# Turning a block of x by DMA by head pairs, and moving the loads of batch 2 behind it

## The chip, the cores and the metric

The kernel runs on one core of one Trainium2 chip. The metric is the device time of one execution in microseconds (us); lower is better. A core has five engines with their own instruction streams: TensorE (PE, the matrix engine; its weight loads are shown as PEld), VectorE (DVE), ScalarE (ACT), GpSimd (POOL) and SyncE (SP). In this kernel SP issues nearly all DMA transfers, and POOL issues most stores of the output.

## The reference

```python
def attn(q, k, v):                     # (8 batches, 8 heads, 576 rows, 64)
    cos, sin = cos/sin(pi/2 * pos / S)
    phi = lambda x: concat([relu(x) * cos, relu(x) * sin], -1)
    kv  = einsum('bhsf,bhsd->bhfd', phi(k), v)
    z   = sum(phi(k), axis=2)
    num = einsum('bhsf,bhfd->bhsd', phi(q), kv)
    den = einsum('bhsf,bhf->bhs', phi(q), z)[..., None] + 1e-06
    return num / den

def moe(x, w_in, w_out, beta):         # x (4608, 512), w_in (512, 2048)
    h = x @ w_in
    g = h * sigmoid(beta * h)
    return g @ w_out                   # (4608, 512)

x = attn(q, k, v).transpose(0, 2, 1, 3).reshape(4608, 512)
out = moe(x, w_in, w_out, beta)
```

## The kernel before

The 4608 tokens are worked on in two tilings at once. The attention goes by batch (8 batches of 576 rows); the two large products go by chunk (9 chunks of 512 tokens). A batch is held as 9 blocks of 64 tokens (n = 0 to 8), with two groups of 64 rows on the 128 partitions, and four head pairs, of which two by two make one of two pair halves (`jp` 0 and 1). A chunk takes 8 blocks: chunk 0 takes batch 0's blocks 0 to 7; chunk 1 takes batch 0's block 8 and batch 1's blocks 0 to 6; chunk 2 begins with batch 1's blocks 7 and 8.

For each batch:

- `load_raw(b, name)` loads q, k or v as float32 on SP's queue (1152 KB each) into one buffer per name, so a load waits until the batch before has been read.
- `q_relu`, `k_relu`, `v_scale` make the bf16 operands: relu of q and k, and v times the cosine and times the sine of the position (`vb`, one row of instructions per block).
- `q_turn_pe` or `q_turn_dma` turns q so that features lie on the partitions (`qts`), by PE or by a DMA transpose; a product with the tangent (`tan_mul`) makes the sine part `qs`.
- `kv_mm` (L276) makes the key-value product in PSUM, `kv_take` copies it out.
- `num_mm` (L297) makes numerator and denominator; `x_rden` (L308, L312) takes the reciprocal of the denominator, and `x_mul` (L319) writes x in bf16 to `xs`.
- `x_turn_pe` (L356, with copies L361 and L363) or `x_turn_dma` (L367) turns x into the chunk's tile `xt`, one tile of 8 blocks by two pair halves.

For each chunk, `h_group` runs 4 matmuls of 512 columns (`h_mm`, L386: two for each pair half) and one activation (`h_act`, L394) for each of 16 column tiles of w_in; then the output product follows. Chunk 0's output is made in the plain way (`o_mm`, L543), chunk 1's and later ones with seven block products in place of eight, which need differences of w_out (`T1` to `T4`, `w_sums`) and sums of g (`S1` to `S4`). `T3` takes the place of a part of w_out that chunk 0's output reads.

The order of the work is written out by hand. Every engine runs its instructions in the order in which they are emitted, and so does SP's queue of DMAs. The slots concerned are these: 32 slots of chunk 0 (4 to 15 finish h, 16 to 31 make the output; slots 24 to 31 take one of the last 8 tiles each) with the dictionary `early` of what is put behind a slot for batch 1; then the 16 slots of chunk 1's h, with the preparation of batch 2 between; then the output of chunk 1 (`o_fast`), with batch 2's numerators and the relu of batch 3's q. Matmuls of a slot go to banks of PSUM (8 of 2 KB) that are named by hand: chunk 1's first four h groups take banks 6, 7, 4, 5, later ones 0, 1, 4, 5 in turn; chunk 0's last outputs are in banks 2, 3, 0, 1.

In the kernel before, batch 1's blocks 0 to 6 are turned by PE (seven transposes at slot 28, seven at slot 29), all three loads of batch 2 are issued at slot 24, and batch 2's key-value product stands behind chunk 1's group 10.

Of the kernel before, what the change touches and what calls it, by code (L numbers as in the profile page):

```python
# [16 lines left out]
P = 128  # L17
# [5 lines left out]
def kernel(  # L23
# [52 lines left out]
    def load_raw(b, name, j0=0, j1=4):  # L76
        js = slice(j0, j1)
        src = {"q": q, "k": k, "v": v}[name][b]
        nc.sync.dma_start(  # L79
            out=raw_tile(b, name)[:, js].rearrange("q j n d -> q j (n d)"),  # L80
            in_=src.rearrange("(j g) (p n) d -> (g p) j (n d)", g=2, n=NQ)[:, js, :])
# [35 lines left out]
    def cast_out(j, eng="d"):  # L117
        i, jj = divmod(j, 4)
        st = stages["out", i]
        if eng == "a":  # L120
            nc.scalar.activation(wout[:, j, :], st[:, jj, :], AF.Copy, scale=rbeta[:, j : j + 1])
        else:
            nc.vector.tensor_scalar(wout[:, j, :], st[:, jj, :],
                                    scalar1=rbeta[:, j : j + 1], scalar2=None, op0=ALU.mult)
# [46 lines left out]
    qs_first = one.tile([P, 2, NQ, P], BF16, name="qs")  # L171
    kv = one.tile([P, 2, 2, 2, E], BF16, name="kv")
    xs = one.tile([P, NQ, 2, 2 * D], BF16, name="xs")

    nc.vector.reciprocal(eps9, cos9)
    nc.vector.tensor_tensor(tan9, eps9, sin9, op=ALU.mult)
# [113 lines left out]
    def num_mm(b, n, jp, bank, slot):  # L290

        for cs in range(2):
            for jj in range(2):
                rows = slice(jj * HP, (jj + 1) * HP)
                for g in range(2):
                    cols = slice(g * HP, (g + 1) * HP)
                    nc.tensor.matmul(  # L297
                        ps[cols, bank + jj, slot * E : (slot + 1) * E],
                        lhsT=(qts[b % 2], qs_of(b))[cs][rows, jp, n, cols],
                        rhs=kv[rows, g, jp, cs, :],  # L300
                        start=(cs == 0), stop=(cs == 1))

    def x_rden(bank, slot, n0, n1, jps):

        w, m = len(jps), n1 - n0
        nv = ps[:, bank : bank + 2, slot * E : (slot + w * m) * E].rearrange("q j (i s e) -> q j i s e", s=w, e=E)
        den = small.tile([P, 2, m, w], FP32, name="den", tag=f"den{m}{w}")
        nc.vector.tensor_tensor(  # L308
            den, nv[:, :, :, :, D],
            eps9[:, n0:n1].unsqueeze(1).unsqueeze(3).to_broadcast([P, 2, m, w]), op=ALU.add)  # L310
        rden = small.tile([P, 2, m, w], FP32, name="rden", tag=f"rden{m}{w}")
        nc.vector.reciprocal(rden, den)  # L312
        return nv, rden, n0, jps

    def x_mul(got, n0, n1):
        nv, rden, first, jps = got
        a, z, w = n0 - first, n1 - first, len(jps)
        o = xs[:, n0:n1, jps[0] : jps[-1] + 1].rearrange("q n s (j d) -> q j n s d", j=2)
        nc.vector.tensor_tensor(  # L319
            o.rearrange("q j n s d -> q j (n s) d"),  # L320
            nv[:, :, a:z, :, 0:D].rearrange("q j n s d -> q j (n s) d"),
            rden[:, :, a:z].rearrange("q j n s -> q j (n s)").unsqueeze(3).to_broadcast([P, 2, (z - a) * w, D]),
            op=ALU.mult)
# [27 lines left out]
    def x_turn_pe(b, n0, n1, bank, engs=("act",), jps=(0, 1)):  # L351
        m, w = n1 - n0, len(jps)
        tv = ps[:, bank].bitcast(BF16)[:, 0 : w * m * P].rearrange("q (n s c) -> q n s c", n=m, s=w)
        for i in range(m):
            for s_, jp in enumerate(jps):
                nc.tensor.matmul(tv[:, i, s_, :], lhsT=xs[:, n0 + i, jp, :], rhs=ident, is_transpose=True,  # L356
                                 start=(i == 0 and s_ == 0), stop=(i == m - 1 and s_ == w - 1))
        for k_, (c, o, a, z) in enumerate(pieces(b, n0, n1)):
            dst, src = xt_tile(c)[:, o : o + z - a, jps[0] : jps[-1] + 1], tv[:, a - n0 : z - n0]
            if engs[k_ % len(engs)] == "act":  # L360
                nc.scalar.copy(dst, src)  # L361
            else:
                nc.vector.tensor_copy(dst, src)  # L363

    def x_turn_dma(b, n0, n1):
        for c, o, n0, n1 in pieces(b, n0, n1):
            nc.sync.dma_start(out=xt_tile(c)[:, o : o + n1 - n0].rearrange("q n s c -> q (n s) c"),  # L367
                              in_=xs[:, n0:n1].rearrange("q n s c -> q (n s c)"), transpose=True)


    gs = {}
# [50 lines left out]
    def wx_tiles():  # L422

        wx["w"] = stage.tile([P, 4, 512], FP32, name="w_stage", tag="w_stage").rearrange("q a f -> q (a f)").bitcast(
            BF16).rearrange("q (k s g f) -> q k s g f", k=4, s=4, g=2)
        wx["v"] = stage.tile([P, 4, 512], FP32, name="w_stage", tag="w_stage").rearrange("q a f -> q (a f)").bitcast(
            BF16).rearrange("q (k s g f) -> q k s g f", k=4, s=4, g=2)
        wx["x"] = stage.tile([P, 4, 512], FP32, name="w_stage", tag="w_stage").rearrange("q a f -> q (a f)").bitcast(
            BF16).rearrange("q (s n c) -> q s n c", s=8, n=NB // 2)
        wx["q"] = stage.tile([P, 4, 512], FP32, name="w_stage", tag="w_stage").rearrange("q a f -> q (a f)").bitcast(  # L430
            BF16)[:, 0 : 2 * NQ * P].rearrange("q (s n c) -> q s n c", s=2, n=NQ)
# [352 lines left out]
    def num_seven(jp, bank):  # L784
        for n in range(7):
            num_mm(1, n, jp, bank, n)
# [3 lines left out]
    def second():  # L790

        takes.append(q_turn_pe(1, 0, 4, hold=True))
        takes.append(q_turn_pe(1, 1, 6, hold=True))
        cast_out(8)
        takes[0]("act", 0)
        takes[0]("dve", 1)
        cast_out(9, "a")
        takes[0]("dve", 0)
        takes[0]("act", 1)
        cast_out(10)  # L800
        for e, i in (("act", 0), ("dve", 1), ("act", 1), ("dve", 0)):
            takes[1](e, i)
        for j in (11, 12, 14, 15):
            cast_out(j, "a")

    early = {
# [1 line left out]
        15: lambda: (v_scale(1, 1, n1=8, eng="act"), k_relu(1, 2, 4, "act")),  # L808
        22: lambda: (kv_mm(1, 0, 6), kv_mm(1, 1, 6), kv_take((0, 1), 6, "act"), q_relu(1, 1, "act", 5)),
        23: second,  # L810
        25: lambda: (num_seven(0, 4), x_mul(x_rden(4, 0, 0, 7, (0,)), 0, 7), cast_out(13)),
        26: lambda: (num_seven(1, 6), x_mul(x_rden(6, 0, 0, 7, (1,)), 0, 7)),
        28: lambda: x_turn_pe(1, 0, 7, 4, ("act",), (0,)),
        29: lambda: x_turn_pe(1, 0, 7, 5, ("dve",), (1,)),
    }

    def num_rest():
        for n in range(7, NQ):
            for jp in range(2):
                num_mm(1, n, jp, 2, 2 * (n - 7) + jp)  # L820
        x_mul(x_rden(2, 0, 7, NQ, (0, 1)), 7, NQ)
        x_turn_dma(1, 7, NQ)

    def att_q(b, turn=True):
        q_relu(b, 0)
# [23 lines left out]
    def x_part(b, t, bank):  # L849
        x_div(t, bank)  # L850
        x_turn_dma(b, 3 * t, 3 * t + 3)

    for slot in range(32):
        if slot < 4:
            if slot == 0:
                for jt in range(2):
                    h_mm(0, jt, (2, 3), slice(0, 4))
            h_mm(0, slot, (2, 3), slice(4 if slot < 2 else 0, 8))
            h_act(0, slot)
        elif slot < 16:  # L860
            h_group(0, slot)
        elif slot < 24:
            o_part(0, slot % 4, (slot - 16) // 4)
        else:
            for tt in range(4):
                o_mm(0, tt, (slot - 16,))
        if slot == 24:
            for name in "qvk":
                load_raw(2, name)
        if slot in early:  # L870
            early[slot]()

    def w_sums():
        z = ALU.subtract
        nc.vector.tensor_tensor(T1, B12, B11, op=z)
        nc.vector.tensor_tensor(T2, B22, T1, op=z)
        nc.vector.tensor_tensor(T4, B21, T2, op=z)
        nc.vector.tensor_tensor(T3, B22, B12, op=z)

    wx_tiles()  # L880
    for slot in range(16):
        h_group(1, slot)
        if slot == 0:
            num_rest()
            att_q(2)
            v_half(2, 0)
        if 2 <= slot < 6:
            v_half(2, 1, slot + 3, slot + 4, "act")
        if slot == 4:
            k_all(2)  # L890
            v_half(2, 1, 0, 5)
        elif slot == 6:
            w_sums()
        elif slot == 10:
            kv_all(2, eng="act")
            for jp in range(2):
                tan_mul(nc.vector, qs_of(2)[:, jp], qts[0][:, jp], 0, NQ)
    q_relu(3, 0, "act")
    q_relu(3, 1, "act")
    q_turn_dma(3)  # L900

    def one_sums(kind):
        for i0 in range(0, JT // 2, 2):
            g_sum(1, i0, i0 + 2, kind)
# [6 lines left out]
    ops(x, "1 c1")  # L911
    one_sums(1)
    ops(y, "1 c1")
    for t, bank in enumerate((4, 6, 0)):
        num_all(2, t, bank)
    one_sums(2)
# [174 lines left out]
```

## Time and profile before

| | |
|---|---|
| median of 3 runs | 274.5 us (274.12 to 275.24) |
| span of the profiled execution, first to last instruction | 272.8 us |
| PE busy | 265.6 us (97%) |
| DVE busy | 224.3 us (82%) |
| ACT busy | 188.6 us (69%) |
| POOL busy | 67.5 us (25%) |
| mean granted TensorE clock | 0.999 |

The profile gives the span and no separate device time of that execution; the median of the runs is 1.7 us above the span. Times in the timelines count from the first instruction. Busy times are of one profiled execution; "L356" is line 356 of the kernel before. A DMA instruction's own time is the time SP took to issue it; when its data have landed is told apart, as "us to landing" from the issue.

### The profile page before, as it was taken

To read this page: it belongs to the slowest core of one execution; us is meant where nothing else is said; L and a number is where in the kernel's file an instruction comes from. 1 tells how busy PE (TensorE), PEld (TensorE's weight loads), DVE (VectorE), ACT (ScalarE), POOL (GpSimd) and SP (SyncE) were. 2 spreads that over 40 slices of the span, in tenths; PEclk is the share of its full clock that TensorE was granted. 3 is DMA by queue.
4 is the path that set the end of the run, shared out by engine and by line. 5 is a ranking of instruction groups with operands and counts; after the bars stand their busy time and mean duration, and the time that the engine had idled before them with its cause. 6 is when DMAs were issued, how large, how long until landed. Compare 5 with 4: busy or idle time off the path is not lost.

```text
span 272.8 us, 8972 instructions
## 1 busy us (share of the span) xinstructions
PE 265.6 (97%) x3712; PEld 207.0 (76%) x3712; DVE 224.3 (82%) x596; ACT 188.6 (69%) x384; POOL 67.5 (25%) x87
## 2 busy tenths in 40 slices
PE   8889999999999999999999999999999999999993
PEld 8554455445874488888888888888888888888882
DVE  5889959499999989789989996999599768748841
ACT  4778777797329656899489967996695179329910
POOL 1454000510078000560094009300930060000000
PEclk9999999999999999999999999999999999999999
DMA  7999999999959999893689339944500460024006
GB/s 221 388 390 377 394 390 312 394 207 344 278 114 331 215 362 258 264 296 67 190 210 353 85 63 244 293 70 83 162 1 8 77 163 2 2 47 110 0 6 151
DMA packets 50745, 54.00 MB, mean 198 GB/s; under 512 B 31232, under 2 KB 31760, under 8 KB 50704
## 3 DMA queue, kind: packets, MB, share of 16 engines
q1 hardware_dynamic: 47664, 45.82, 59.1%
q0 software_dynamic: 2688, 7.34, 9.2%
q8 instruction: 29, 0.48, 0.7%
q10 hardware_dynamic: 352, 0.27, 0.4%
q14 instruction: 12, 0.10, 0.1%
HBM read 36.71 MB, written 9.44 MB: 169 GB/s over the span
## 4 chain that ended last, share of the span: by engine, by line
PE 91%; DMA 3%; DVE 2%; SPq 1%; issue 1%
PE ps L620 32%; PE ps L511 27%; PE ps L386 15%; PE ps L543 5%; PE ps L562 5%; PE ps L297 4%; DMA raw_v<-in_v_dram 3%; PE ps L276 3%; DVE xs L319 1%; SPq L79 1%; PE ps L356 0%; PE ps L235 0%; DVE win L115 0%; DVE rden L312 0%; DVE vb L209 0%
## 5 line engine op out<-in xcount | busy, mean ns | idle before, releaser
L420 ACT ACTIVATE g_t<-ps,beta 128x512 bf16<-128x512 f32 x96 | 60.4, 704 | 1.4 <-PE ps L511 1.3
L536 POOL DMA_DIRECT2D out_dram<-o_sb x56 | 32.9, 594 | 103.7 <-ACT o_sb L657 44.0
L620 PEld LDWEIGHTS <-S 128*128 128x128 bf16 x448 | 43.4, 98 | 5.2
L511 PE MATMUL ps<-w_stage 128*128 128x256 bf16 x288 | 46.6, 272 | 0.1
L386 PE MATMUL ps<-xt,win 128*128 128x512 bf16 (+1 forms) x196 | 42.8, 375 | 0.1
L511 PEld LDWEIGHTS <-w_stage 128*128 128x128 bf16 x384 | 37.3, 98 | 5.1 <-issue 0.3
L487 DVE TENSOR_TENSOR ps<-ps,p 128x256 f32<-128x256 f32 x74 | 30.5, 427 | 8.6 <-PE ps L511 3.0
L394 ACT ACTIVATE g_t<-ps,beta 128x512 bf16<-128x512 f32 x48 | 32.3, 689 | 7.2 <-PE ps L386 7.1
L620 PEld LDWEIGHTS <-g_t 128*128 128x128 bf16 x336 | 32.3, 98 | 4.5 <-ACT g_t L420 0.4
L386 PEld LDWEIGHTS <-win 128*128 128x128 bf16 x196 | 18.8, 98 | 21.0 <-issue 0.4
L511 PE MATMUL ps<-xt,win 128*128 128x256 bf16 x192 | 32.9, 273 | 0.0
L511 PEld LDWEIGHTS <-win 128*128 128x128 bf16 x288 | 28.0, 98 | 3.5
L620 PE MATMUL ps<-wout,g_t 128*128 128x256 bf16 x224 | 28.9, 273 | 0.0
L406 DVE TENSOR_TENSOR S<-g_t 128x512 bf16<-128x512 bf16 (+1 forms) x66 | 25.7, 418 | 2.6 <-ACT g_t L420 1.7
L480 ACT COPY ps<-ps 128x256 f32<-128x256 f32 x62 | 22.6, 384 | 7.5 <-PE ps L620 4.0
L217 ACT ACTIVATE vb<-raw_v,sin 128x256 bf16<-128x256 f32 (+1 forms) x58 | 26.0, 505 | 2.5 <-DMA raw_v<-in_v_dram 2.5
L620 PE MATMUL ps<-T,S 128*128 128x256 bf16 x224 | 26.6, 273 | 0.0
L620 PE MATMUL ps<-wout,S 128*128 128x256 bf16 x224 | 26.4, 273 | 0.0
L319 DVE TENSOR_TENSOR xs<-ps,rden 128x768 bf16<-128x768 f32 (+4 forms) x26 | 22.8, 883 | 0.9 <-DVE rden L312 0.2
L223 POOL TENSOR_TENSOR qs<-qt,tanr 128x1152 bf16<-128x1152 bf16 x6 | 14.3, 2391 | 27.4 <-PE ps L562 21.0
L219 DVE TENSOR_SCALAR vb<-raw_v,cos 128x256 bf16<-128x256 f32 x63 | 20.3, 371 | 0.0
L657 ACT COPY o_sb<-ps 128x512 f32<-128x512 f32 x11 | 6.3, 587 | 20.1 <-PE ps L620 20.1
(112 smaller groups left out, 410.7 us busy)
## 6 DMA issues: line engine op xcount, KB each, us to landing
raw_v<-in_v_dram SPq DMA_DIRECT2D x7, 1152.0 KB, 9.7
raw_k<-in_k_dram SPq DMA_DIRECT2D x7, 1152.0 KB, 9.4
raw_q<-in_q_dram SPq DMA_DIRECT2D x7, 1152.0 KB, 7.4
out_dram<-o_sb POOLq DMA_DIRECT2D x56, 128.0 KB, 4.7
w_stage<-in_moe_w_in_dram SPq DMA_DIRECT2D x3, 1024.0 KB, 13.2
w_stage<-in_moe_w_out_dram SPq DMA_DIRECT2D x2, 1024.0 KB, 8.0
w_stage<-in_moe_w_out_dram SPq DMA_DIRECT2D x4, 512.0 KB, 11.9
out_dram<-o_sb SPq DMA_DIRECT2D x12, 128.0 KB, 2.4
```

The lines of the kernel that those rows point to most:

```text
L217: got = nc.scalar.activation(o, a, AF.Copy, scale=t[:, n : n + 1])
L219: got = nc.vector.tensor_scalar(o, a, scalar1=t[:, n : n + 1], scalar2=None, op0=ALU.mult)
L319: nc.vector.tensor_tensor(o.rearrange("q j n s d -> q j (n s) d"), nv[:, :, a:z, :, 0:D].rearrange("q j n s d -> q j (n s) d"), rden[:, :, ...
L386: nc.tensor.matmul(ps[:, h_bank(c, jt), i * 64 : (i + w) * 64], lhsT=win[jt // 4][:, mi, (jt % 4) * P : (jt % 4 + 1) * P], rhs=xt[:, i : i ...
L394: return nc.scalar.activation(gs[c, jt // 4][:, jt % 4], ps[:, h_bank(c, jt)], AF.Silu, scale=beta[:, jt : jt + 1])
L406: return nc.vector.tensor_tensor(o, l, r, op=op)
L420: return nc.scalar.activation(gs[c, jt // 4][:, jt % 4], bank, AF.Silu, scale=beta[:, jt : jt + 1])
L480: return nc.scalar.copy(at("a", 0), at("b", 0))
L487: nc.vector.tensor_tensor(dst, at("b", 0), st["p5"], op=ALU.add)
L511: nc.tensor.matmul(dst, lhsT=l[:, g], rhs=r[:, :, g * HP : (g + 1) * HP], start=start and g == 0, stop=g == 1, skip_group_check=True)
L536: (eng or own).dma_start(out=out_v[bb, n][:, m0:m1], in_=o_sb[hf * HP : (hf + 1) * HP, m0:m1])
L620: nc.tensor.matmul(dst, lhsT=l(i), rhs=r[:, i], start=start and i == 0, stop=i == order[-1], skip_group_check=True)
```

## The change

Batch 1's blocks 0 to 6 of x are turned by two DMA transposes, one for each pair half, instead of 14 transposes on PE. `x_mul` writes them to `x_pairs`, a view of the same buffer in which the seven blocks of a pair half lie together. The order around it is written anew:

- of batch 2's loads only the first half of q is issued at slot 24; the second half of q, v and k are issued after the second pair turn (slot 26);
- the numerators of batch 1's blocks 7 and 8 (`num_rest`) move from chunk 1's slot 0 to chunk 0's slot 28, into banks 4 and 5; their turn stays at chunk 1's slot 0 on SP;
- the first relu of batch 2's q and three of the four weight differences move to slot 29, the fourth difference to chunk 1's slot 0;
- the scaling of w_out's column tile 13 moves from DVE to ACT;
- chunk 1's h begins with the two matmuls of pair half 0 for the first four tiles, followed by those of pair half 1;
- in chunk 1 the sine rows of v on ACT move from slots 2 to 5 to slots 6 to 9, the relu of k with v's other sine rows on DVE from slot 4 to 6, and the key-value product from slot 10 to 12;
- batch 3's q relu and turn move from ahead of chunk 1's output product to behind its first two sub-products.

```diff
--- before.py
+++ after.py
@@ -171,6 +171,7 @@
     qs_first = one.tile([P, 2, NQ, P], BF16, name="qs")
     kv = one.tile([P, 2, 2, 2, E], BF16, name="kv")
     xs = one.tile([P, NQ, 2, 2 * D], BF16, name="xs")
+    x_pairs = xs[:, 0:7].rearrange("q n s c -> q (n s c)").rearrange("q (s n c) -> q n s c", s=2, c=P)
 
     nc.vector.reciprocal(eps9, cos9)
     nc.vector.tensor_tensor(tan9, eps9, sin9, op=ALU.mult)
@@ -312,10 +313,10 @@
         nc.vector.reciprocal(rden, den)
         return nv, rden, n0, jps
 
-    def x_mul(got, n0, n1):
+    def x_mul(got, n0, n1, to=xs):
         nv, rden, first, jps = got
         a, z, w = n0 - first, n1 - first, len(jps)
-        o = xs[:, n0:n1, jps[0] : jps[-1] + 1].rearrange("q n s (j d) -> q j n s d", j=2)
+        o = to[:, n0:n1, jps[0] : jps[-1] + 1].rearrange("q n s (j d) -> q j n s d", j=2)
         nc.vector.tensor_tensor(
             o.rearrange("q j n s d -> q j (n s) d"),
             nv[:, :, a:z, :, 0:D].rearrange("q j n s d -> q j (n s) d"),
@@ -366,6 +367,11 @@
         for c, o, n0, n1 in pieces(b, n0, n1):
             nc.sync.dma_start(out=xt_tile(c)[:, o : o + n1 - n0].rearrange("q n s c -> q (n s) c"),
                               in_=xs[:, n0:n1].rearrange("q n s c -> q (n s c)"), transpose=True)
+
+
+    def x_turn_pair(jp):
+
+        nc.sync.dma_start(out=xt_tile(1)[:, 1:NB, jp], in_=x_pairs[:, :, jp], transpose=True)
 
 
     gs = {}
@@ -800,7 +806,7 @@
         cast_out(10)
         for e, i in (("act", 0), ("dve", 1), ("act", 1), ("dve", 0)):
             takes[1](e, i)
-        for j in (11, 12, 14, 15):
+        for j in (11, 12, 13, 14, 15):
             cast_out(j, "a")
 
     early = {
@@ -808,18 +814,18 @@
         15: lambda: (v_scale(1, 1, n1=8, eng="act"), k_relu(1, 2, 4, "act")),
         22: lambda: (kv_mm(1, 0, 6), kv_mm(1, 1, 6), kv_take((0, 1), 6, "act"), q_relu(1, 1, "act", 5)),
         23: second,
-        25: lambda: (num_seven(0, 4), x_mul(x_rden(4, 0, 0, 7, (0,)), 0, 7), cast_out(13)),
-        26: lambda: (num_seven(1, 6), x_mul(x_rden(6, 0, 0, 7, (1,)), 0, 7)),
-        28: lambda: x_turn_pe(1, 0, 7, 4, ("act",), (0,)),
-        29: lambda: x_turn_pe(1, 0, 7, 5, ("dve",), (1,)),
+        25: lambda: (num_seven(0, 4), x_mul(x_rden(4, 0, 0, 7, (0,)), 0, 7, x_pairs), x_turn_pair(0)),
+        26: lambda: (num_seven(1, 6), x_mul(x_rden(6, 0, 0, 7, (1,)), 0, 7, x_pairs), x_turn_pair(1),
+                     load_raw(2, "q", 2, 4), load_raw(2, "v"), load_raw(2, "k")),
+        28: lambda: num_rest(),
+        29: lambda: (q_relu(2, 0), w_sums(0)),
     }
 
     def num_rest():
         for n in range(7, NQ):
             for jp in range(2):
-                num_mm(1, n, jp, 2, 2 * (n - 7) + jp)
-        x_mul(x_rden(2, 0, 7, NQ, (0, 1)), 7, NQ)
-        x_turn_dma(1, 7, NQ)
+                num_mm(1, n, jp, 4, 2 * (n - 7) + jp)
+        x_mul(x_rden(4, 0, 7, NQ, (0, 1)), 7, NQ)
 
     def att_q(b, turn=True):
         q_relu(b, 0)
@@ -849,6 +855,15 @@
     def x_part(b, t, bank):
         x_div(t, bank)
         x_turn_dma(b, 3 * t, 3 * t + 3)
+
+    def w_sums(part):
+        z = ALU.subtract
+        if part == 0:
+            nc.vector.tensor_tensor(T1, B12, B11, op=z)
+            nc.vector.tensor_tensor(T2, B22, T1, op=z)
+            nc.vector.tensor_tensor(T4, B21, T2, op=z)
+        else:
+            nc.vector.tensor_tensor(T3, B22, B12, op=z)
 
     for slot in range(32):
         if slot < 4:
@@ -865,40 +880,35 @@
             for tt in range(4):
                 o_mm(0, tt, (slot - 16,))
         if slot == 24:
-            for name in "qvk":
-                load_raw(2, name)
+            load_raw(2, "q", 0, 2)
         if slot in early:
             early[slot]()
 
-    def w_sums():
-        z = ALU.subtract
-        nc.vector.tensor_tensor(T1, B12, B11, op=z)
-        nc.vector.tensor_tensor(T2, B22, T1, op=z)
-        nc.vector.tensor_tensor(T4, B21, T2, op=z)
-        nc.vector.tensor_tensor(T3, B22, B12, op=z)
-
     wx_tiles()
+    for jt in range(4):
+        h_mm(1, jt, (0, 1))
     for slot in range(16):
-        h_group(1, slot)
+        if slot < 4:
+            h_mm(1, slot, (2, 3))
+            h_act(1, slot)
+        else:
+            h_group(1, slot)
         if slot == 0:
-            num_rest()
-            att_q(2)
+            x_turn_dma(1, 7, NQ)
+            q_relu(2, 1)
+            q_turn_dma(2)
+            load_raw(3, "q")
+            w_sums(1)
             v_half(2, 0)
-        if 2 <= slot < 6:
-            v_half(2, 1, slot + 3, slot + 4, "act")
-        if slot == 4:
+        if 6 <= slot < 10:
+            v_half(2, 1, slot - 1, slot, "act")
+        if slot == 6:
             k_all(2)
             v_half(2, 1, 0, 5)
-        elif slot == 6:
-            w_sums()
-        elif slot == 10:
+        elif slot == 12:
             kv_all(2, eng="act")
             for jp in range(2):
                 tan_mul(nc.vector, qs_of(2)[:, jp], qts[0][:, jp], 0, NQ)
-    q_relu(3, 0, "act")
-    q_relu(3, 1, "act")
-    q_turn_dma(3)
-
     def one_sums(kind):
         for i0 in range(0, JT // 2, 2):
             g_sum(1, i0, i0 + 2, kind)
@@ -911,6 +921,9 @@
     ops(x, "1 c1")
     one_sums(1)
     ops(y, "1 c1")
+    q_relu(3, 0, "act")
+    q_relu(3, 1, "act")
+    q_turn_dma(3)
     for t, bank in enumerate((4, 6, 0)):
         num_all(2, t, bank)
     one_sums(2)
```

## The prediction

> **What bounds the kernel now.** I read the page first, then the chain of waits in order of time around chunk 1's start, then the timelines of SP and DVE there, then the transfers of single windows. From the page, busy time and the chain by engine:
>
> ```profile
> PE 265.6 (97%) x3712; PEld 207.0 (76%) x3712; DVE 224.3 (82%) x596; ACT 188.6 (69%) x384; POOL 67.5 (25%) x87
> ...
> PE 91%; DMA 3%; DVE 2%; SPq 1%; issue 1%
> ```
>
> From 19 us on PE has hardly a gap: what leaves PE is gained, and whatever PE waits for is lost, since nothing later can catch it up. The chain (start, us, what) where the change works:
>
> ```profile
> 47.33 0.39 PE ps L356 x7
> ...
> 48.58 0.39 PE ps L356 x7
> ...
> 50.70 0.86 PE ps L386 x4
> 51.56 0.38 PE ps L297 x30
> ...
> 60.68 1.15 PE ps L276 x72
> ```
>
> L356 are the 14 transposes of x; at 50.70 chunk 1's h begins, 0.864 us for a group of four matmuls; at 60.68 batch 2's key-value product (72 matmuls). Nobody is waited for. SP's timeline (start, us to issue) shows when batch 2's loads leave:
>
> ```profile
> 40.79 0.37 SPq L79 DMA_DIRECT2D raw_q<-in_q_dram  x1
> 41.22 0.49 SPq L79 DMA_DIRECT2D raw_v<-in_v_dram  x1
> 41.76 0.51 SPq L79 DMA_DIRECT2D raw_k<-in_k_dram  x1
> 53.25 2.21 SPq L367 DMA_TRANSPOSE xt<-xs  x1
> ...
> 60.26 0.53 SPq L79 DMA_DIRECT2D raw_q<-in_q_dram  x1
> ```
>
> Asked for the window of that third issue, the transfers say (KB, us to landing)
>
> ```profile
> raw_k<-in_k_dram SPq DMA_DIRECT2D x1, 1152.0 KB, 14.1
> ```
>
> so k is there at 55.9. DVE's timeline uses it almost at once:
>
> ```profile
> 44.88 1.09 DVE L319 TENSOR_TENSOR xs<-ps,rden 128x896 bf16<-128x896 f32 x1
> ...
> 46.75 1.09 DVE L319 TENSOR_TENSOR xs<-ps,rden 128x896 bf16<-128x896 f32 x1
> ...
> 56.84 1.35 DVE L193 TENSOR_SCALAR rk<-raw_k 128x2304 bf16<-128x2304 f32 x1
> 58.11 1.40 DVE L219 TENSOR_SCALAR vb<-raw_v,sin 128x256 bf16<-128x256 f32 x5
> ```
>
> The product at 60.68 has its last operand at 59.5: 1.2 us to spare. This cover is what the change touches.
>
> **The change part by part.** Sums are made against the profiled execution, span 272.8 us; the median of the timed runs is 274.5, and the 1.7 us around the span are taken as unchanged.
>
> PE's saving: 14 transposes go, 0.39 + 0.39 = 0.78 us, all on the path. Their copies (0.91 us on ACT, 0.62 on DVE) were off it.
>
> The two turns by DMA: pair 0's product on DVE ends at 45.97, pair 1's at 47.84, less 0.39 for the weight scaling at 45.88 that goes to ACT: 47.45. No seven-block turn is in the trace. The nearest are six blocks, 1.25 us to issue and 2.8 to land (median of L367): scaled by 7/6, 1.46 us and some 3.0. Pair 0 lands at 49.0, pair 1 at 50.5. The far end is the turn at 53.25 behind loads: 6.3 us for four blocks. I take 3.0, because only half of q (576 KB) is still ahead and at the loads' rate is through by 46.3. Need: h begins at 50.70 - 0.78 + 0.38 (the last two blocks' numerators now come ahead) = 50.3, and its pair-1 half four times two matmuls later, 52.0. Spare 1.3 and 1.5 us: no cost. That h goes by pairs changes no count of matmuls; the first four activations then come due 0.43 us apart where one takes 0.66, which ACT makes good before their banks are wanted again.
>
> At nothing, with cover: the numerators of blocks 7 and 8 in banks 4 and 5 (free at 45.97; 0.38 us of PE moved, not added) and their division (DVE is idle between 47.84 and 49.01 and from 49.6 to 52.1); q's first relu and three of the weight differences (0.7 + 3 x 1.23 us) into that gap and up to 53; the scaling on ACT (0.64 us, into the idle 0.93 before 47.75). The two-block turn moves behind the loads on SP, but chunk 2 reads it only at 80.
>
> The loads. q's second half, v and k leave SP after the pair-1 turn, at 47.45 + 1.46 = 48.9 instead of 40.8 to 42.3. After a turn loads start slowly; these windows follow the issue at 60.26 (last two columns DMA share and GB/s):
>
> ```profile
> 61.50:62.00 0.50, 0.50 (x26) 0.29 (x15) 0.47 (x2) 0.07 (x1) 0.00 (x0) 1.00 0.83 72
> 62.00:62.50 0.50, 0.50 (x4) 0.26 (x3) 0.50 (x1) 0.50 (x1) 0.00 (x0) 1.00 0.54 152
> 62.50:63.00 0.50, 0.50 (x4) 0.21 (x3) 0.50 (x1) 0.19 (x2) 0.00 (x0) 1.00 1.03 378
> ```
>
> This is as if full rate began 1.9 us after the issue: here 50.8. The bytes are 576 + 1152 + 1152 KB = 2.95 MB; alone at 390 GB/s 7.6 us. But POOL's eight stores of chunk 0 (128 KB each, issued from 50.98, first packets some 2 us later) now fall on top of them; before, the loads were over by 54. How the two share is seen in the transfers of 115 to 118, with both active:
>
> ```profile
> q0 software_dynamic: 241, 0.67, 55.8%
> q1 hardware_dynamic: 246, 0.56, 47.0%
> ```
>
> Stores 223 GB/s, loads 187. So 2.0 us alone (0.78 MB), 4.7 us beside 1.05 MB of stores (0.88 MB), and 1.29 MB alone in 3.3: k's bytes end at 60.8. Landing came later than the bytes by 0.3 (q), 1.1 (the q at 60.26) and 1.9 us (k) in the trace; I take 1.1: k lands at 61.9; v's bytes, by the same shares, end at 57.8, so it lands at 58.9. Bounds: 59.5 if stores gave way wholly, 62.7 with the 1.9.
>
> The Trainium skill ("DMA: Bandwidth & Descriptors", Specifications) gives one core about 358 GB/s from HBM; by that the loads alone would take 8.2 us and the total would be 0.7 us longer, 277.2 us. The trace loads at 388 to 397 in its first full slices, and the sum goes by that.
>
> The wait. The product is moved from behind group 10 to behind group 12: 50.3 + 13 x 0.864 = 61.5, and would end at 62.65. It needs the k relu (pitch 1.27) and the five sine rows of v on DVE (1.31), in this order: 61.9 + 2.6 = 64.5. The product goes block by block, and the fifth block's row comes last; after it 0.6 (only the second pair and a tail) to 1.15 us (all of it) remain, I take 0.9: it ends at 65.4, a wait of 2.75 us. Behind it on PE stand groups 13 to 15 and all of chunk 1's output: all of it moves. k landing at 59.1 costs nothing, at 59.9 the saving is used up. On ACT the first sine row is queued behind group 6's activation (57.1) and waits for v until 58.9, holding up group 7's; its bank is wanted at 59.8: at most 0.4 us, and it lies ahead of the longer wait, so it is not added.
>
> Late next: q's turn, issued behind the loads, lands at about 65.6; the tangent products (2.6 us) end at 68.2, and the numerators need them at 65.4 + 2.6 + 1.75 = 69.8. The sums S1, S2 follow on DVE to 71 as PE gets there. Batch 3's q relu is queued behind both first copies (70 on ACT) and its q, which leaves SP once batch 2's turn is out at 64, lands at about 70: its turn leaves at 72.6 instead of 69.1, behind it the turns of x for chunk 2, the second landing at 81.4. Chunk 2 begins at 79.98 + 2.0: 0.6 us to spare.
>
> Sum: -0.78 + 2.75 = +2.0 us, 276.5. With k's bounds (a wait of 0.4 to 3.6): 274.1 to 277.3.
>
> **Rivals.** *The loads come in time.* The two groups by which the product was put off, and DVE's emptier list, cover the delay; stores yield, or the loads run between the turns. For it: bytes alone end at 58.4, and k landing at 59.1 is free. Against it: stores and loads share evenly at 115 to 118. It gives 274.5 - 0.8 = 273.7, not slower.
>
> *The delay goes round to chunk 2.* A q turn takes 4.3 to 12 us to issue in this trace, and the turns of x stand behind batch 3's on SP; if that takes the median 8.2 instead of 4.9, the second turn lands at 84.7 and chunk 2's first matmul waits 2.7 us: 279.2. For it: 10.7 and 11.7 us where loads and stores were both under way. Against: the one at 69.10, in nearly the same place, took 4.3.
>
> *The pair turns are late.* With 6.3 us instead of 3.0, pair 0 lands at 52.3, h begins 2 us late, and the loads behind move by as much, which takes the place of the first wait and does not add to it: k at 63.7, 278.3. Against: nothing bulky stands ahead of them.
>
> **How the numbers follow.** Forecast 0.57, loads in time 0.23, round to chunk 2 0.11, turns late 0.06; 0.03 for a gain above 1.4 us that I see no source for, since PE's saving is 0.8. 0.5% is 1.4 us, about what a measurement of this kernel can tell from no change. Of the forecast's span of waits some four fifths lie above +1.4: slower 0.47 + 0.17 = 0.64; same 0.10 + 0.23 = 0.33; faster 0.03. The range 273.5 to 278.8 takes in the loads in time, the forecast and most of the late turns; the likeliest case alone has 274.1 to 277.3.
>
> **What would show it.** Right: no L356 in chunk 1; x turns landed before h begins near 50.3; k landing near 62; PE idle ahead of L276, released by DVE, for over 2 us. Wrong: k landing before 59.5, or no gap ahead of L276; PE idle at the first L386 of chunk 1 instead; or a gap at chunk 2's first L386.

## The result, and the profile after

The changed kernel takes 285.5 us (median of four runs, 282.6 to 290.2), the kernel before 274.3 in the same session (273.9 to 275.2). The ratio is 1.036, interval 1.032 to 1.039; the run at 290.2 was disturbed and is left out of it. The forecast was 276.5, 273.5 to 278.8: the direction is right, the size is not.

The profiled execution took 284.56 us, its span is 282.8 instead of 272.8. From the page, busy time and the chain by engine (shares of the span):

```profile
PE 269.3 (95%) x3698; PEld 207.7 (73%) x3698; DVE 223.0 (79%) x594; ACT 187.8 (66%) x384; POOL 66.1 (23%) x87
...
PE 79%; DMA 13%; DVE 4%; issue 2%; SPq 1%
```

PE has 14 matmuls fewer and is busy 3.7 us longer, and DMAs stand in the chain with 13% (4.7 of it is the load of batch 2's k). The chain of waits in order of time says where (start, us, what):

```profile
50.45 13.21 DMA raw_k<-in_k_dram
...
66.41 0.99 PE ps L277 x56
67.40 4.36 PE ps L392 x12
71.76 1.75 PE ps L568 x16
73.51 1.20 PE ps L298 x119
74.71 2.83 issue
...
77.98 12.06 PE ps L568 x96
```

The line numbers have moved by 1 or 6: L277 is the key-value product, L392 h, L298 the numerators, L568 the output products. Three things are new. The path waits for k until 63.66. Behind the product, 12 matmuls of h take 4.36 us where 0.216 each (0.864 for four) makes 2.59; at full clock the experiments show 2.69 to 2.70 in this place. And inside batch 2's numerators PE stands still for 2.83 us with nothing to wait for that the profile shows ("issue"); the 96 output products behind it take 12.06 us, in the kernel before 10.59. Chunk 2 begins at 90.05 instead of 80.15, and from there to the end the two kernels take the same time, 192.75 and 192.65 us.

SP's timeline, and the transfers in the window of the third load (KB, us to landing):

```profile
45.68 3.57 SPq L374 DMA_TRANSPOSE xt<-xs  x2
49.30 0.57 SPq L79 DMA_DIRECT2D raw_q<-in_q_dram  x1
...
50.45 0.51 SPq L79 DMA_DIRECT2D raw_k<-in_k_dram  x1
```

```profile
raw_k<-in_k_dram SPq DMA_DIRECT2D x1, 1152.0 KB, 13.2
```

k lands at 63.65; before, at 55.9. PE's timeline shows the product (in brackets the idle time before it, and who ended it):

```profile
65.36 2.04 PE L277 MATMUL ps<-vb,rk 64*64 64x130 bf16 x72 [2.83 <-DVE vb L220]
```

It is released by the value rows that DVE scales after the k relu, as the forecast had it, and takes 2.04 us instead of 1.15 because the rows come one by one. The windows (us, then PE, PEld, DVE, ACT, POOL busy; the last three columns are granted clock, DMA share, GB/s):

```profile
68.00:69.00 1.00, 1.00 (x3) 0.30 (x2) 1.00 (x2) 0.09 (x1) 0.00 (x0) 0.50 0.93 318
69.00:70.00 1.00, 1.00 (x4) 0.44 (x3) 0.89 (x3) 0.69 (x1) 0.00 (x0) 0.50 1.04 410
75.00:77.50 2.50, 0.00 (x0) 0.00 (x0) 2.43 (x8) 1.03 (x1) 0.00 (x0) 1.00 0.31 99
78.50:79.50 1.00, 1.00 (x7) 0.72 (x5) 1.00 (x4) 0.00 (x0) 0.00 (x0) 0.50 1.14 217
```

The first, second and fourth: after the wait for the product and after the stop in the numerators TensorE works at half the granted clock. The third is the stop in the numerators itself: PE and PEld at nothing. For 72.5 to 77.5 the transfers list one more queue (packets, MB, share):

```profile
q8 instruction: 1, 0.02, 1.3%
```

The page counts 29 such packets, 0.48 MB, so 16 KB each. PE and PEld have 3698 instructions each, 7396 together, 255 for each packet: each packet seems to hold the next 256 instructions of TensorE, at 64 bytes. To the microsecond they start at 48, 53, 66, 71 and 80 us before, and at 46, 56, 75 and 80 after: the one at 75 begins 0.3 us after PE stopped and takes 1.04, and PE resumes 1.5 us behind it.

### The profile page after: what moved, and what is told of

Its sections match the earlier page's. It is cut to its first block, busy times and chain, and to the rows that moved or that the text cites. A ratio compares the mean times of both kernels' runs of the same rounds, so it can differ in the third digit from the quotient of the medians.

```text
span 282.8 us, 8949 instructions
## 1 busy us (share of the span) xinstructions
PE 269.3 (95%) x3698; PEld 207.7 (73%) x3698; DVE 223.0 (79%) x594; ACT 187.8 (66%) x384; POOL 66.1 (23%) x87
## 4 chain that ended last, share of the span: by engine, by line
PE 79%; DMA 13%; DVE 4%; issue 2%; SPq 1%
PE ps L626 31%; PE ps L517 26%; PE ps L392 8%; DMA raw_q<-in_q_dram 5%; PE ps L568 5%; DMA raw_k<-in_k_dram 5%; PE ps L298 4%; DMA raw_v<-in_v_dram 3%; PE ps L277 3%; PE ps L549 2%; SPq L79 1%; DVE xs L320 1%; DVE rk L194 1%; PE ps L236 0%; DVE win L115 0%
## 5 line engine op out<-in xcount | busy, mean ns | idle before, releaser
L542 POOL DMA_DIRECT2D out_dram<-o_sb x56 | 31.5, 571 | 105.9 <-ACT o_sb L663 44.3
L392 PE MATMUL ps<-xt,win 128*128 128x512 bf16 (+1 forms) x196 | 44.6, 385 | 1.0 <-ACT g_t L400 0.9
L392 PEld LDWEIGHTS <-win 128*128 128x128 bf16 x196 | 19.2, 100 | 23.7 <-issue 3.9
L220 DVE TENSOR_SCALAR vb<-raw_v,cos 128x256 bf16<-128x256 f32 x63 | 19.3, 356 | 3.4 <-DMA raw_v<-in_v_dram 3.4
```

The lines of the kernel that those rows point to most:

```text
L220: got = nc.vector.tensor_scalar(o, a, scalar1=t[:, n : n + 1], scalar2=None, op0=ALU.mult)
L392: nc.tensor.matmul(ps[:, h_bank(c, jt), i * 64 : (i + w) * 64], lhsT=win[jt // 4][:, mi, (jt % 4) * P : (jt % 4 + 1) * P], rhs=xt[:, i : i ...
L542: (eng or own).dma_start(out=out_v[bb, n][:, m0:m1], in_=o_sb[hf * HP : (hf + 1) * HP, m0:m1])
```

## The experiments

Two theories stood at the start. One: everything comes from the late k (idle time, then half the clock). The other: the late k makes about half, and the rest is a fetch boundary of TensorE's instructions, which 28 instructions fewer (14 transposes and their weight loads) have moved into the numerators, where 256 instructions last only 1.3 us (73.44 to 74.71). None of the kernels leaves work out; warm_pe(n, c) issues n matmuls of c columns whose results nobody reads, and stands in both kernels as the warm-up at the start. Each time is set against runs of the kernel before on the same chip, medians 274.3 to 274.9.

**Fourteen matmuls more in the warm-up (e1).**

```
-    warm_pe(58, 48)
+    warm_pe(72, 48)
```

> The changed kernel with 14 more small matmuls in the warm-up at the very start, where PE waits for the first loads: PE's instruction stream is shifted back by 28 instructions, as long as it was with the 14 transposes. Theory (fetch): the 2.8 us in which PE stands still inside batch 2's numerators (74.7 to 77.5) is a wait for the next 16 KB of PE's instructions, whose boundary has moved to the start of the numerators, where 256 instructions last 1 us only. Then this gap goes, and with it the half clock behind it (1.5 us): 281.2 us. Rival (traffic): the gap comes from loads of batch 3 standing in the way of whatever PE needs there: it stays, 285.5 us. Rival (operand): PE waits there for the tangent product or the turned q: it stays, 285.5 us.

278.7 us, ratio 1.015 (1.012 to 1.019). The chain at the numerators:

```profile
72.42 0.66 issue
73.08 0.45 PE ps L298 x27
73.53 10.59 PE ps L568 x96
```

The stop has shrunk from 2.83 to 0.66 us and the output products are at full clock. It brings 6.8 us, where 4.3 was expected: behind the wait for k (idle 2.35 us here) the clock was not halved either (12 matmuls of h in 2.70), which is 1.7. Against it stands a new stop of 0.79 us at 43.79, in batch 1's numerators.

**The rest of the change without the DMA turns (e2).** x is turned by PE again, all of batch 2's loads leave at slot 24; the reorders stay.

```
-  25: ... x_mul(..., x_pairs), x_turn_pair(0)
-  26: ... x_mul(..., x_pairs), x_turn_pair(1), load_raw(2, "q", 2, 4), load_raw(2, "v"), load_raw(2, "k")
+  25, 26: ... x_mul(...);  28, 29: + x_turn_pe(1, 0, 7, 6 / 7, ...)
+  slot 24: load_raw(2, "q", 2, 4); load_raw(2, "v"); load_raw(2, "k")
```

> The changed order, but blocks 0 to 6 of x turned by PE again and all of batch 2's loads issued at slot 24. Theory (late loads): k lands near 56, PE doesn't wait ahead of the key-value product, and the new order of the preparation costs nothing: 274.3 us, within 0.7. Rival (order): the later key-value product, the sine rows behind slot 6 and batch 3's later turn cost by themselves: 277 us or more.

274.9 us, ratio 1.002 (1.000 to 1.005), span 273.0: no wait before the product, no stop over 0.3 us. The reorders, moved scaling and h by pairs cost nothing that can be measured.

**The loads first, the turns behind them (e3).** DMA turns as in the change, the loads issued at slot 24 as before.

> The changed kernel with all of batch 2's loads issued at slot 24, ahead of the pair turns. Theory (one queue in order): the pair turns land behind 3.5 MB, at 55 to 57, PE waits 5 to 7 us at chunk 1's first matmul, its clock is halved for some us after it, and the wait ahead of the key-value product goes: 281 to 286 us. Rival (the turns pass the loads, or share with them): they land by 52, 274 to 276 us.

286.2 us, ratio 1.041 (1.037 to 1.045). The chain:

```profile
46.20 14.51 DMA xt<-xs
...
80.57 0.46 issue
```

The turns take 10.7 us to issue on SP, land at 60.7, and PE waits 10.4 us for x: longer than the 5 to 7 expected. The two sets of transfers do not fit beside each other in either of the two orders tried. The last line matters for the other theory: PE has the same instructions in the same order as in the changed kernel, and it stops at the same count of them in the numerators, but for 0.46 us instead of 2.83. Here the DMA engines carry nothing from 78.0 to 78.6, and the packet of instructions starts at 78.60, 2.0 us before the stop; in the changed kernel their share is 1.04 to 1.13 from 71 to 75, and the packet starts 0.3 us after PE has stopped. So the boundary says where PE stops; how long it stands goes with how early the packet gets through, and the first experiment's rival "traffic" is not out as far as the length is concerned. No run varies the traffic alone.

**Late loads without the DMA turns (e4).** x turned by PE, the loads issued behind the turn of blocks 7 and 8, at 51.0 to 52.2.

> As e2 (x turned by PE), but q's second half, v and k are issued only behind the turn of blocks 7 and 8, near 49.3 us, as late as in the changed kernel, and with one turn of four blocks ahead of them in place of fourteen. Theory (late loads): the lateness alone makes PE wait ahead of the key-value product, by 2 to 4 us less the 0.8 by which PE comes later, and halves its clock: 278 to 282 us. Rival (the DMA turns themselves slow the loads or PE): without them there is little to see, 274 to 276 us.

281.3 us, ratio 1.024 (1.022 to 1.027). The chain:

```profile
52.15 12.72 DMA raw_k<-in_k_dram
...
69.29 3.64 PE ps L392 x12
74.67 1.36 PE ps L298 x135
```

Lateness costs 6.8 us here without any DMA turn of these blocks (the loads leave 1.7 later still than in the change), 1.6 of it as half clock (0.67 in the rest of the product, 0.95 in the h behind it; the wait itself is 2.29 us, with one of 1.18 on ACT ahead of it); the numerators run through, and PE has its 14 transposes.

**PE kept busy during the wait (e5).**

```
-    warm_pe(58, 48)
+    warm_pe(45, 48)
...
+            warm_pe(13, 512, bank=2)
             kv_all(2, eng="act")
```

> The changed kernel with 13 idle matmuls of 512 columns (2.8 us at full clock, into a bank that nobody reads) put behind group 12, where PE stands waiting for the key-value product's operands, and 13 fewer in the warm-up, so that PE's stream is as long as before it. Theory (the wait halves the clock): with PE kept busy there the clock stays at full speed, and the last three groups take 2.6 us instead of 4.4: 283.7 us, 1.8 less than the changed kernel. Rival (the groups were slow for another reason, such as their weights or x arriving late): they stay at 4.4 us, 285.5 us.

Behind the wait the clock stays full (12 matmuls of h in 2.69 us, idle 0.8), as expected of this step. The total is no better: 287.1 us, ratio 1.044 (1.040 to 1.048), since the shorter warm-up moved the boundaries again: stops of about 2 us in the start-up and of 3.21 in the numerators, with 13.27 us for the output products.

**The kernel before with a shorter warm-up (e8).** The other theory by itself: nothing of the change in it.

```
-    warm_pe(58, 48)
+    warm_pe(44, 48)
```

> The kernel before with 14 fewer small matmuls in the warm-up: nothing else is touched, PE's instruction stream is 28 shorter ahead of batch 2's numerators, as in the changed kernel. Theory (fetch): the 16 KB boundary falls at the start of the numerators, and PE stands still there for 1.5 to 3 us: 276 to 278 us. Rival (the gap needs late loads or a shifted order): nothing happens, 274.5 us.

281.5 us, ratio 1.024 (1.021 to 1.027), and the chain shows the same picture at the same place:

```profile
69.72 1.24 PE ps L297 x118
70.96 2.97 issue
73.93 0.32 PE ps L297 x15
74.25 12.25 PE ps L562 x96
```

Work was taken out at the start, and the kernel became 6.7 us slower: 2.97 + 1.66 here, and about 1.5 in the start-up. This settles that moving the boundaries does it without the late loads and without the rest of the change; how busy the DMA engines are at that moment still counts, as e3 showed.

**Fourteen matmuls more in the kernel before, ahead of chunk 0's first h (e11).**

> The kernel before with 14 small matmuls more in the same place, where PE waits anyway. Theory (fetch): the 0.24 us stall that its numerators show at 68.9 and a part of the slow matmuls around it go: 274.0 to 274.4 us. Rival (that stall is no fetch, or others come up): 274.5 us or more.

280.4 us, ratio 1.019 (1.015 to 1.023), a miss: batch 2's numerators run through, but now batch 1's stop for 3.10 us at 44.20, and the start-up for 1.00. The kernel before lies at a favourable position; the one shift tried to each side loses.

**Stores out of the loads' way (e6).** With the 72 of the first experiment, chunk 0's eight stores go to SP behind the load of batch 3's q.

> e1 (changed kernel with 14 matmuls more in the warm-up) with chunk 0's eight stores issued by SP behind batch 2's q turn and batch 3's q load instead of by POOL from 50. Theory (bytes): v and k then have the DMA engines to themselves, k lands 2 to 2.7 us sooner, near 60.8, and the wait ahead of the key-value product shrinks from 2.7 to under 1 us: 276.5 us. Rival (the ring, not the bytes): the loads are slow because of the start behind the turns and not because of the stores: k lands no sooner, 278.7 us.

280.1 us, ratio 1.019 (1.014 to 1.023), a miss in the total. The wait for k is nearly gone, as the theory had it (k relu at 60.06, product at 62.4), but PE waits 3.6 us for x at chunk 2: batch 3's turn and the turns of x stand behind the stores on SP. This is the prediction's second rival, made by hand. With the sine rows moved ahead of the k relu as well (e7):

> e6 with DVE's five sine rows of v put ahead of the relu of k, so that only 1.35 us of DVE work is left once k has landed, and the product runs at its full pace of 1.15 us. If the wait of e6 is gone: PE's saving of 0.8 us is left, 273.7 to 274.5 us. If k lands after 61.5 even so: 275 to 276 us.

281.1 us, ratio 1.023 (1.019 to 1.027), a miss again. The product runs at full pace, 1.15 us, so the one-by-one rows do account for its 2.04; the wait for x at chunk 2 stays (3.0), and stops of 0.7 and 1.15 us in the numerators come on top.

**Twenty-four matmuls ahead of chunk 0's first h, in the changed kernel (e9).**

> The changed kernel with 24 more small matmuls (48 columns) ahead of chunk 0's first h, where PE waits for DVE, so that the first 2500 PE instructions keep the place they have in the kernel before and the boundary ahead of batch 2's numerators lies in the slower matmuls before them. Theory (fetch and late loads, two separate costs): the gap in the numerators and the clock loss behind it go, the wait for k stays: 277 to 279 us, the late loads' own price being +3 to +4. Rival (the late loads make the gap too): 282 us or more.

281.1 us, ratio 1.025 (1.023 to 1.026), a miss by 2: the numerators run through (10.59 us for the output products), but a stop of 1.97 us comes into the start-up. k's wait is 2.5 us, h behind it 4.36. The same with the stores on SP and batch 3's turn behind those of x (e10):

> e9 with chunk 0's stores on SP behind batch 3's q load, as in e6, and batch 3's q turn put on SP behind the turns of x for chunk 2, which in e6 came 3.8 us too late because they stood behind that q turn and the stores. If nothing new comes late: PE's saving of 0.8 us is left, 273.7 to 274.6 us, at or under the kernel before. If batch 3's loads, now behind the stores, hold up chunk 2 in another place: 275 to 277 us.

281.3 us, ratio 1.024 (1.020 to 1.028), a miss: no wait for x and 1.2 us for k, but a stop of 1.85 us in the start-up with half the clock behind it, one of 0.65 in the numerators, and batch 3's value rows late (DVE stands for 1.36 us at 92).

**Fourteen matmuls just ahead of chunk 1 (e12).** Nothing ahead of that place moves.

```
+        30: lambda: warm_pe(14, 48, bank=6),
```

> The changed kernel with 14 matmuls of 48 columns (some 0.4 us, into a bank nobody reads) behind chunk 0's slot 30, about where the 14 transposes were: PE's stream has its old length from there on and the start of the program is untouched. Theory (two costs): no gap in batch 2's numerators and no slow matmuls behind them, the wait for k with its slow matmuls stays: 280 to 281.5 us, so 4 to 5 us of the loss are the boundary's and 6 the late loads'. Rival (the gap follows the late loads wherever the boundary lies): 285 us.

278.8 us, ratio 1.015 (1.012 to 1.018), better than the 280 to 281.5 expected. The chain:

```profile
49.96 12.41 DMA raw_k<-in_k_dram
...
66.52 3.91 PE ps L392 x12
...
72.18 1.36 PE ps L298 x138
73.54 10.59 PE ps L568 x96
```

No stop, full clock on the output products, and the wait for k as before it (idle 2.5 us, half clock behind). Chunk 2 begins at 84.13, 5.92 us earlier than in the changed kernel: 2.83 the stop, 1.47 the output products, 0.28 the numerators, 0.45 h; the product ends 0.88 earlier, as k landed 1.3 earlier and the padding takes 0.4.

**The same with chunk 0's stores on SP behind batch 3's loads, and batch 3's turn behind those of x (e13).**

> e12 with chunk 0's stores issued by SP behind batch 3's k and v loads, and batch 3's q turn behind the turns of x for chunk 2. If the wait for k goes and nothing else comes late: 274 to 275 us, the transposes' 0.8 us less the padding's 0.4. If the DMA work that the turns add has to come late somewhere: a new wait at the product of batch 3 or at chunk 2's first matmul, 276 to 278 us.

277.6 us, ratio 1.012 (1.009 to 1.015), the best with the DMA turns, and still slower than before. The wait for k is 0.5 us (the product again in 2.04), the clock stays full, chunk 2 waits for nothing; but the stores take 10.9 us to issue on SP, batch 3's sine rows come late, and a later value load is 10.0 us under way with 0.9 us of waiting on PE at 109.6.

## Why the prediction was wrong

Its sum beside the trace, from the start of chunk 1's h to that of chunk 2's (us):

| step | forecast | measured |
|---|---|---|
| h of chunk 1 begins | -0.4 (50.3) | -0.6 (50.1) |
| numerators of blocks 7 and 8 no longer inside | -0.38 | -0.38 |
| the product's end later than by its place | +2.75 | +4.92 |
| 12 matmuls of h behind it (4.36 against 2.69) | 0 | +1.67 |
| stop in the numerators | 0 | +2.83 |
| output products | 0 | +1.47 |
| sum | +2.0 | +9.9 |

The h start is read from PE's timeline, 49.93 against 50.53, on the chain's scale 50.10 against 50.70; the product's place is 50.10 + 13 x 0.864 + 1.15 = 62.48, and it ends at 67.40. Between the starts of chunk 2 lie 9.9 us, 90.05 against 80.15.

Right: the saving on PE; the pair turns, 3.5 and 3.0 us to landing (3.0 forecast), at 49.2 and 51.0, where h wants them at 50.1 and 51.8, with no wait; the reorders at nothing (the PE-turned version, 1.002); the product held by k through DVE; chunk 2 not held. The hold on ACT was more than its bound (0.94 us at 60.5 instead of 0.4) and was swallowed by the longer wait, as the step said.

Mis-sized: "k lands at 61.9"; it was 63.65, beyond the upper bound of 62.7. Pair 0's turn took 2.23 us to issue and pair 1's 1.29, where 1.46 was taken for each, so that the loads left at 49.3 instead of 48.9. Full rate came at 52, not 50.8, and did not last: with k's load long issued,

```profile
52.00:53.00 1.00, 1.00 (x7) 0.44 (x5) 1.00 (x1) 0.71 (x2) 1.00 (x3) 1.00 1.14 376
53.00:54.00 1.00, 1.00 (x6) 0.43 (x5) 0.00 (x0) 1.00 (x2) 1.00 (x3) 1.00 0.93 290
54.00:55.00 1.00, 1.00 (x6) 0.48 (x5) 0.71 (x2) 1.00 (x3) 1.00 (x2) 1.00 0.94 290
```

The sum had 390 there. The sharing with the stores was as forecast; the transfers of 57 to 60 show

```profile
q0 software_dynamic: 251, 0.67, 56.4%
q1 hardware_dynamic: 255, 0.56, 47.4%
```

From k's landing to the product's end it is 3.75 us, forecast 3.5. So 2.2 us of the miss are this one term.

Left out, first: what a wait does to the clock behind it. The sum took the wait for its own length. Behind the 2.83 us of idle the granted clock is 0.50 from 67.32 to 70.73, for 3.41 us, which costs 1.67; with PE fed during the wait (e5) the clock is not halved there (12 matmuls in 2.69). The Trainium skill ("TensorE: Matmul & The Clock Gate", Part 1) says that TensorE falls to half its clock after an idle window of about 3.4 us, which runs freely, and comes back after about 3.4 us of work. The half clock and the length of the slow stretch agree: in all the traces the slow stretches between start and end are 3.4 us long or two or three times that. The idle time needed was less here, and its length does not decide alone: 1.85 (e10), 2.29 (e4), 2.5 (e12) and 2.83 us did it, 2.35 (e1) and 3.55 us (e6) did not. A window that runs freely would explain that, since the same idle time can lie in one window or be split over two; no run varies this by itself. The forecast wait of 2.75 us is under the page's figure and within what the traces show, so a half-clock term should have been in the range.

Left out, second, and the larger: that taking instructions away moves the fetch boundaries of those behind. The step "14 transposes go, 0.78 us, all on the path" was right as PE time and costs 4.3 us by the stop in the numerators and the half clock behind it. The kernel before with 14 warm-up matmuls fewer shows this without the change (281.5), the padded one takes it away (278.8).

That the stop is a wait for the fetch shows when the traces are counted through. The changed kernel and its experiments have 22 stops of PE of 0.25 us or more with no releaser ("issue"). Counting two instructions for each weight load begun before PE resumes, all 22 lie 180 to 190 places past a multiple of 256, whether in the start-up, in the numerators of batch 1 or 2, or later. And in all 22 the last 16 KB packet had ended 1.24 to 1.52 us before PE went on, whether the stop was 0.26 or 3.21 us long.

The Trainium skill ("Runtime: NRT & Kernel Launch", Instruction fetch mechanics) describes the 256-instruction blocks, fetched on a queue of the engine's own, and calls the cost of a boundary "mostly hidden". At most boundaries of these traces it is; in the numerators it was up to 3.2 us, and the measurement decides.

The prediction's signs for right came true but the landing near 62 (the second turn landed at 51.0, after h began but before h wanted it), and none of its signs for wrong did: they spoke of DMA waits alone. No rival had either left-out term.

Open: why k landed 1.3 us earlier in the version padded ahead of chunk 1 than in the changed kernel, with the same loads (0.5 of it is the load's earlier issue, 49.96 against 50.45); what besides the length of the idle time decides whether the clock falls; and how much of a stop's length is the traffic, as no run varies that alone. No view names the fetch as the releaser; it is shown by the count, by the packets' times and by the shifts.

## What to carry to other kernels

Cost a load that is moved not by its bytes alone, but by what else is in the queues when it lands, and give it a margin; a wait on TensorE of about 2 us or more can cost 1.7 us again, as half the clock for the next 3.4. When an edit changes the number of TensorE's instructions, look for "issue" gaps in its densest stretches of small matmuls before judging the edit: a few padding matmuls just ahead of the stretch tell whether the loss belongs to the edit or to where the fetch boundaries fell. A trade of PE work for DMA work pays only where the queue and the DMA engines have room for it; here 0.8 us of PE came back as a wait for whatever transfer stood behind.

## What the runs showed of the hardware

- TensorE's instructions arrive in packets of 16 KB (256 instructions) on the DMA engines. 28 instructions fewer at the start made an otherwise unchanged kernel 2.4% slower.
- A late packet shows only as "issue": 2.83, 2.97 and 3.21 us in batch 2's numerators, where 288 instructions (144 matmuls and their weight loads) run in about 1.5 us, 3.10 us in batch 1's, and 0.46 us in e3, where the DMA engines were free before it. PE goes on 1.24 to 1.52 us after the end of the packet.
- Idle times of 1.85 to 3.21 us halved the granted clock behind them, mostly for 3.4 us; others of 1.97 (e9), 2.35 and 3.55 us did not.
- A DMA turn of seven blocks behind all of batch 2's loads on the same queue (e3): 4.5 and 6.1 us to issue, 11.4 and 14.5 to landing; with little ahead of it (the changed kernel) 1.3 and 2.2, 3.0 and 3.5.
